# Sparse attention and an FFN on one core: attention pairs taken two to a slot, with one attention head of the slot

## The chip, the cores and the metric

The kernel runs on one core of a Trainium2 chip. Its metric is the device time of one execution in microseconds. A profile of one execution shows when each engine worked: PE (TensorE, matmuls and transposes), DVE (VectorE), ACT (ScalarE), POOL (GpSimd) and SP (SyncE, which here only issues DMAs; POOL issues DMAs too).

## The reference

Attention over q, k, v of 8 batches, 8 heads, 576 positions and 64 elements, then an FFN on the 4608 tokens of 512 features that it gives. Heads 0 to 3 see a window of 32 positions, heads 4 to 7 every 32nd position.

```python
scores = scale * np.matmul(q, k.transpose(0, 1, 3, 2))
rel = pos[:, None] - pos[None, :]
mask_local = (rel >= 0) & (rel < stride)                                   # heads 0 to 3
mask_strided = (rel >= 0) & (pos[None, :] % stride == pos[:, None] % stride)   # heads 4 to 7
scores = np.where(masks, scores, -1e9)
attn = softmax(scores)
x = (attn @ v), heads side by side          # 4608 x 512
h = (x @ w1) * (x @ w2) @ w3                # d_ff = 1024
out = h @ w_out                             # 4608 x 512, float32
```

## The kernel before

**Work and its units.** Two heads of a batch make a pair, 32 in all, four to a batch: pairs 0 and 1 of a batch are local, 2 and 3 strided. A pair goes through these steps, each a function:

- `load_qk` and `load_v` bring q, k and v in (q and k, and the strided v, through POOL's queue; the local v through SP's). `emit_cast_v` casts the local v on POOL, and `shift_v` makes a copy of it that is shifted by 32 rows, with two DMAs on SP's queue.
- `emit_T`: TensorE transposes q and k (36 transposes for a local pair, 44 for a strided one) into the two PSUM buffers of pool `psA`; the copies to SBUF go to ACT, but the strided q goes to DVE.
- `emit_S`: scores (36 or 22 small matmuls) into two buffers of `psF`, and the mask added by two DVE operations.
- `emit_max`, `emit_sub` (DVE), `emit_exp` (ACT), `emit_norm`: sum and reciprocal on DVE (L371, L373), product on POOL (L374).
- `emit_P`: the probabilities transposed. `by_dma` decides: strided pairs from `XB` = 8 on use a DMA transpose on SP's queue (L388), the others TensorE (`pp`, 5 transposes for a local pair, 6 for a strided one) and a copy on ACT.
- `emit_V`: probabilities times v (36 or 22 matmuls) into two `psF` buffers, copied into `xT` by ACT, and for strided pairs by ACT once and DVE twice.

The FFN works on 9 chunks of 512 tokens. w3 and w_out are folded into one matrix `wfh` at the start. `emit_a` and `emit_b` are four matmuls of 128x512 each, eight times per chunk; ACT copies the result of a to `asb`, DVE multiplies it with that of b into `abt` (L256). `emit_out` makes a tile of 128 tokens with eight matmuls; ACT copies it to `osb` and SP sends it.

`psF` has six buffers (PSUM banks) for scores, values and all FFN results; a new tile takes the bank that was released first.

**Order.** The program's order is written out by hand, engine by engine in the order of the calls (`tc.manual_schedule()`). Pairs 0 to 8 have a prologue of single calls. From pair 9 on a loop does one step for each pair n:

```python
for n in range(9, NP + 2):
    ...
    if by_dma(n - 1):
        emit_P(n - 1)
    ...
    emit_S(n); emit_V(n - 2); emit_T(n + 1)      # one attention block on TensorE
    feed(0.1 * f, first)                          # f = 5.2
    emit_max(n); feed(...); emit_sub(n); emit_exp(n); feed(...)
    ...
```

`feed` puts FFN pieces in between: it adds its microseconds to a credit and emits pieces (0.87 for an a or b, 1.74 for an output tile) until the credit is used up; `next_piece` decides which, and only from batches that are done (`first`, `full`). An output tile of a chunk may come when two more pieces of the next chunk are out, or when no a or b is possible. When the loop ends, `feed(1e9, B)` emits all that is left.

Of the kernel before, what the change touches and what calls it, by code (L numbers as in the profile page):

```python
# [27 lines left out]
def kernel(  # L28
# [11 lines left out]
    nc = tc.nc  # L40
# [30 lines left out]
    NP, XB = 4 * B, 8  # L71
    staged, cast, qks, prs, pts = {}, {}, {}, {}, {}
# [143 lines left out]
    abts, aqs = {}, {}  # L216
# [41 lines left out]
    def emit_out(c, ts):  # L258
        ps = psF.tile([P, DM], FP32, tag="f", name="ops")
        for jc in range(KC2):  # L260
            nc.tensor.matmul(ps, abts[c][:, jc, ts * P:(ts + 1) * P], wfh[:, jc, :],  # L261
                             start=(jc == 0), stop=(jc == KC2 - 1))
        osb = ffn.tile([P, DM], FP32, tag="osb", bufs=3, name="osb")
        nc.scalar.copy(out=osb, in_=ps)  # L264
        nc.sync.dma_start(out_r[c * (NT // P) + ts], osb)

# [16 lines left out]
    def emit_T(i, qeng=nc.scalar.copy):  # L283
# [4 lines left out]
        tps = [psA.tile([P, nsl, npar], FP16, tag="tr", name=f"tp{n}") for n in "qk"]  # L288
# [6 lines left out]
        if local:  # L295
            kT = kTL[par]
            qT = att.tile([P, LB, HALF], FP16, tag="qT", name="qT")
            for dst, off, tp in ((qT, 0, tps[0]), (kT, QB, tps[1])):
                eng = qeng if dst is qT else nc.scalar.copy
                eng(out=_sub(dst, 0, P, off, [[LB, HALF], [1, LB]]),  # L300
                    in_=_sub(tp, 0, P, 0, [[1, HALF], [HALF, LB]]))
        else:
            qT = qTS[par]
            kT = att.tile([P, ST * SW], FP16, tag="kT", name="kT")
            nc.vector.tensor_copy(out=qT[:, :, 0:SW], in_=tps[0])
            nc.scalar.copy(out=kT, in_=tps[1].rearrange("p t k -> p (t k)"))
        qks[i] = (qT, kT)

    def emit_S(i):

        b, hp, local, par = where(i)
        qT, kT = qks.pop(i)
        nt, w = (LB, LW) if local else (ST, SW)
        tmp = att.tile([P, nt, w], FP32, tag="tmp", name="tmp")
        n1 = 5 if local else 6
        sps = [psF.tile([P, n, w], FP32, tag="f", name="sp") for n in (n1, nt - n1)]
        for s in [x for u in range(n1) for x in (u, n1 + u) if x < nt]:
            bank, t = divmod(s, n1)
            for h in range(2):
# [10 lines left out]
                nc.tensor.matmul(sps[bank][c:c + HALF, t, :], qT[r, T, :], kT[r, SW * T:SW * T + w], start=True, stop=True)  # L330
        for bank, (t0, t1) in enumerate(((0, n1), (n1, nt))):
            if local:
                msk = maskL[:, 0:5, :] if t0 == 0 else maskL[:, 1:5, :]
            else:
                msk = _sub(maskS, 0, P, 0, [[0, t1 - t0], [1, SW]])
            nc.vector.tensor_tensor(out=tmp[:, t0:t1, :], in0=sps[bank], in1=msk, op=ALU.add)  # L336
        prs[i] = tmp

# [27 lines left out]
    def emit_norm(i):  # L366
# [6 lines left out]
        nc.vector.reciprocal(out=rc, in_=sm)  # L373
        nc.gpsimd.tensor_tensor(out=prv, in0=prv, in1=_sub(rc, 0, P, 0, [[1, nt], [0, w]]),  # L374
                                op=ALU.mult)

# [22 lines left out]
    def emit_V(i):  # L399
        b, hp, local, par = where(i)  # L400
        vv, pT = pts.pop(i)
        x0 = S * b
        if local:
            ops = [psF.tile([P, LC - half, HALF], FP32, tag="f", name="op") for half in range(2)]
# [12 lines left out]
            for half in range(2):  # L417
                nc.scalar.copy(out=_sub(xT[hp], 0, P, x0 + HALF * half,
                                        [[P, LC - half], [1, HALF]]), in_=ops[half])
        else:  # L420
            ops = [psF.tile([P, 6 - half, SW], FP32, tag="f", name="op") for half in range(2)]
            for s in range(6):
                for half in range(2):
# [3 lines left out]
                    for h in range(2):  # L427
# [5 lines left out]
            nc.scalar.copy(out=_sub(xT[hp], 0, P, x0, [[NR, NA], [11, 3], [1, 6]]),  # L433
                           in_=_sub(ops[0], 0, P, 0, [[3, NA], [1, 3], [SW, 6]]))
            nc.vector.tensor_copy(out=_sub(xT[hp], 0, P, x0 + 6, [[NR, NA], [11, 2], [1, 5]]),
                                  in_=_sub(ops[1], 0, P, 0, [[3, NA], [1, 2], [SW, 5]]))
            nc.vector.tensor_copy(out=_sub(xT[hp], 0, P, x0 + 28, [[NR, NA], [1, 4]]),  # L437
                                  in_=_sub(ops[1], 0, P, 2, [[3, NA], [SW, 4]]))
# [6 lines left out]
    T_A = 0.87  # L445
    state = {"credit": 0.0, "ab": 0, "out": 0, "turn": 0}

    def next_piece(batches):
# [5 lines left out]
        can_out = oc < NCH and a >= 2 * KC2 * (oc + 1) + (0 if c >= NCH else 2)  # L454
# [38 lines left out]
    with tc.manual_schedule():  # L493
# [186 lines left out]
        for n in range(9, NP + 2):  # L680
            full = (n - 1) // 4
            first = full - 1 if n % 4 == 1 else full
            f = 5.2
            if n + 4 < NP:
                load_qk(n + 4)
            for i in (n + 3, n + 2):
                if i < NP and where(i)[2] == (i == n + 3):
                    load_v(i)
            if by_dma(n - 1):
                emit_P(n - 1)  # L690
            if n < NP:
                shift_v(n)
            if n < NP:
                emit_S(n)
            emit_V(n - 2)
            if n + 1 < NP:
                emit_T(n + 1)
            feed(0.1 * f, first)
            if n < NP:
                emit_max(n)  # L700
            feed(0.15 * f, first)
            if n < NP:
                emit_sub(n)
                emit_exp(n)
            feed(0.15 * f, full)
            if n <= NP and not by_dma(n - 1):
                emit_P(n - 1)
# [38 lines left out]
```

## Time and profile before

| | |
|---|---|
| median of 3 runs | 281.21 us (280.95 to 281.38) |
| the profiled execution | 281.55 us, of which the profile's span is 279.8 |
| PE busy | 263.6 us, 94% |
| DVE, ACT, POOL busy | 172.4, 150.5, 159.1 us |
| chain that ended last | PE 66%, DMA 8%, POOL 7%, issue 7%, DVE 6%, ACT 3% |

A line of the profile names the source line, engine and operation, the written and read tiles, the shape and the count. Busy time is that of the engine. In order of time the first number is the start in us from the span's start, the second the length, and in brackets stand the idle time before it and what ended that. A matmul's length is that of its way through the array; successive matmuls overlap, so TensorE's pace is read from one start to the next.

### The profile page before, as it was taken

Reading aid. Unit: us, or ns where it says so; the run is one execution under the profiler, and the core shown is the slowest. Engines: PE = TensorE matmul, PEld = TensorE weight load, DVE = VectorE, ACT = ScalarE, POOL = GpSimd, SP = SyncE. Lnnn points to the kernel's source line nnn. Section 1 sums busy time; section 2 is a strip of 40 time slices with the busy share of each in tenths; the row PEclk is TensorE's granted clock in tenths of the full one; section 3 lists DMA queues with packets and bytes.
Section 4 is the critical chain, followed back from the end, with each engine's and each line's share of the span. In section 5 each row is a group of like instructions: output and inputs, shape, how many; then the busy total and the mean of one; then the engine's idle time right before and its main releaser. Section 6 shows DMA issues by size and latency. Waiting matters only on the chain.

```text
span 279.8 us, 10171 instructions
## 1 busy us (share of the span) xinstructions
PE 263.6 (94%) x4355; PEld 138.4 (49%) x4355; DVE 172.4 (62%) x342; ACT 150.5 (54%) x270; POOL 159.1 (57%) x242
## 2 busy tenths in 40 slices
PE   6479988899999999999999999999999999999994
PEld 6436545454555555545554555455455544444441
DVE  3515664498778867876777688587867841331310
ACT  3324466457676666655675666576656534324322
POOL 7763875779398588557757755895977110000000
PEclk9957999999999999999999999999999999999999
DMA  7999699979779599668957986995674213001113
GB/s 137 189 201 223 93 149 203 152 132 200 157 144 196 75 195 232 71 102 199 229 67 110 224 178 74 166 226 96 75 185 87 30 45 135 0 0 53 63 62 125
DMA packets 59981, 36.95 MB, mean 132 GB/s; under 512 B 38180, under 2 KB 54304, under 8 KB 59936
## 3 DMA queue, kind: packets, MB, share of 16 engines
q0 software_dynamic: 23392, 17.29, 43.3%
q1 hardware_dynamic: 36544, 19.01, 26.6%
q8 instruction: 34, 0.56, 0.8%
q14 instruction: 11, 0.09, 0.1%
HBM read 39.24 MB, written 9.44 MB: 174 GB/s over the span
## 4 chain that ended last, share of the span: by engine, by line
PE 66%; DMA 8%; POOL 7%; issue 7%; DVE 6%; ACT 3%; SPq 1%; POOLq 0%; DVEq 0%; ACTq 0%
PE ops L261 19%; PE bps L253 17%; PE aps L243 16%; PE fps L233 4%; DMA vhL<-vhL 3%; DMA w3s<-in_moe_w_dram 3%; DMA pT<-prS 2%; POOL s L105 2%; DVE abt L256 2%; PE tpk L292 2%; PE tpq L292 1%; PE pp L393 1%; PE op L429 1%; POOL vhS L130 1%; PE op L413 1%
## 5 line engine op out<-in xcount | busy, mean ns | idle before, releaser
L256 DVE TENSOR_TENSOR abt<-bps,asb 128x512 f16<-128x512 f32 x72 | 49.4, 686 | 42.1 <-PE bps L253 39.9
L253 PE MATMUL bps<-xT,w2h 128*128 128x512 f16 x288 | 74.1, 380 | 0.0
L243 PE MATMUL aps<-xT,w1h 128*128 128x512 f16 x288 | 74.0, 379 | 0.0
L261 PE MATMUL ops<-wfh,abt 128*128 128x512 f16 x288 | 65.5, 379 | 0.0
L247 ACT COPY asb<-aps 128x512 f32<-128x512 f32 x72 | 42.2, 587 | 33.9 <-PE aps L243 33.7
L264 ACT COPY osb<-ops 128x512 f32<-128x512 f32 x36 | 21.1, 587 | 42.6 <-PE ops L261 40.3
L261 PEld LDWEIGHTS <-abt 128*128 128x128 f16 x288 | 27.4, 98 | 32.0
L130 POOL DMA_DIRECT2D vhS<-in_v_dram x70 | 42.0, 665 | 1.1 <-issue 1.1
L253 PEld LDWEIGHTS <-w2h 128*128 128x128 f16 x288 | 26.8, 98 | 30.4
L243 PEld LDWEIGHTS <-w1h 128*128 128x128 f16 x288 | 27.0, 98 | 29.6 <-DVE xT L437 0.4
L374 POOL TENSOR_TENSOR prS<-prS,rc 128x594 f16<-128x594 f16 x16 | 19.5, 1220 | 37.0 <-ACT asb L247 26.1
L374 POOL TENSOR_TENSOR prL<-prL,rc 128x576 f16<-128x576 f16 x16 | 19.0, 1187 | 18.5 <-DVE rc L373 16.9
L351 DVE TENSOR_TENSOR tmp<-tmp,mx 128x576 f32<-128x576 f32 (+1 forms) x32 | 25.5, 797 | 1.0
L105 POOL DMA_DIRECT2D s<-in_k_dram x35 | 22.5, 719 | 3.9 <-DMA w2h<-in_moe_w_dram 2.9
L344 DVE TENSOR_REDUCE mx<-tmp 128x9 f32<-128x576 f32 (+1 forms) x32 | 24.0, 752 | 0.2
L233 PE MATMUL fps<-woh,w3T 128*128 128x512 f16 x64 | 18.8, 426 | 4.2 <-issue 1.6
L105 POOL DMA_DIRECT2D s<-in_q_dram x35 | 21.7, 654 | 1.5 <-DMA w1h<-in_moe_w_dram 1.5
L336 DVE TENSOR_TENSOR tmp<-sp,maskL 128x320 f32<-128x320 f32 (+1 forms) x32 | 13.1, 450 | 13.8 <-PE sp L324 13.8
L292 PE MATMUL tpq<-id,s 54*64 54x54 f16 (+1 forms) x640 | 17.1, 194 | 2.3 <-DMA s<-in_q_dram 2.3
L371 DVE TENSOR_REDUCE sm<-prL 128x9 f32<-128x576 f16 x16 | 12.0, 753 | 10.8 <-ACT prL L363 10.8
L292 PE MATMUL tpk<-id,s 54*64 54x54 f16 (+1 forms) x640 | 17.7, 195 | 0.2
L292 PEld LDWEIGHTS <-s 54*64 54x64 f16 (+1 forms) x1280 | 14.8, 108 | 6.0 <-DMA s<-in_q_dram 2.9
(75 smaller groups left out, 296.8 us busy)
## 6 DMA issues: line engine op xcount, KB each, us to landing
out_dram<-osb SPq DMA_DIRECT2D x36, 256.0 KB, 3.1
vsL<-in_v_dram SPq DMA_DIRECT2D x32, 128.0 KB, 4.9
s<-in_k_dram POOLq DMA_DIRECT2D x16, 144.0 KB, 4.1
s<-in_q_dram POOLq DMA_DIRECT2D x16, 144.0 KB, 3.9
s<-in_q_dram POOLq DMA_DIRECT2D x31, 74.2 KB, 4.6
s<-in_k_dram POOLq DMA_DIRECT2D x31, 74.2 KB, 4.9
w3s<-in_moe_w_dram POOLq DMA_DIRECT2D x4, 512.0 KB, 10.2
vhL<-vhL SPq DMA_DIRECT2D x16, 120.0 KB, 5.2
```

What stands on the lines that cost most here:

```text
L105: nc.gpsimd.dma_start(t[p0 + r0[0]:p0 + r0[1], h, 0:n * D], _ap(src[b, h0 + h], 0 + ap[0], ap[1] + [[1, n * D]]))
L130: nc.gpsimd.dma_start(vt[HALF * half + r0[0]:HALF * half + r0[1], h, 0:m * D], _ap(v[b, h0 + h], 6 * half * D + ap[0], ap[1] + [[1, m * D]]))
L233: nc.tensor.matmul(ps, w3T[:, kc, :], woh[:, kc, :], start=(kc == 0), stop=(kc == KC2 - 1))
L243: nc.tensor.matmul(aps, w1h[:, ci, jc * P:(jc + 1) * P], xT[ci][:, c * NT:(c + 1) * NT], start=(ci == 0), stop=(ci == KC1 - 1))
L247: nc.scalar.copy(out=asb, in_=aps)
L253: nc.tensor.matmul(bps, w2h[:, ci, jc * P:(jc + 1) * P], xT[ci][:, c * NT:(c + 1) * NT], start=(ci == 0), stop=(ci == KC1 - 1))
L256: nc.vector.tensor_mul(abts[c][:, jc, :], bps, abts.pop((c, jc)))
L261: nc.tensor.matmul(ps, abts[c][:, jc, ts * P:(ts + 1) * P], wfh[:, jc, :], start=(jc == 0), stop=(jc == KC2 - 1))
L292: nc.tensor.transpose(tp[HALF * h:HALF * h + HALF, s, :], s16[p0:p0 + npar, h, s * D:(s + 1) * D], id16[p0:p0 + npar, p0:p0 + npar])
L344: nc.vector.tensor_reduce(out=mx, in_=tmp, axis=AX.X, op=ALU.max)
L351: nc.vector.tensor_tensor(out=tmp, in0=tmp, in1=_sub(mx, 0, P, 0, [[1, nt], [0, w]]), op=ALU.subtract)
L374: nc.gpsimd.tensor_tensor(out=prv, in0=prv, in1=_sub(rc, 0, P, 0, [[1, nt], [0, w]]), op=ALU.mult)
```

## The change

The step for each pair is replaced from pair 11 on. `emit_T`, `emit_S`, `emit_norm` and `emit_V` are split into their matmuls and the copies or operations that follow (`mm_T`, `evict_T`, `mm_S`, `emit_mask`, `emit_sum`, `emit_div`, `mm_V`, `evict_V`). A slot takes a local and a strided pair together, and a string `STEADY` gives the order of its calls: first letter the step, second letter the pair (L or S), and at the end the engine of a copy (a for ACT, d for DVE); f and g are feeds of 0.29. `now` is the slot's two pairs (scores to probabilities), `old` those of the slot before (values), `new` those of the next (q and k transposed), `far` those three slots on (q and k loaded). On TensorE a slot starts with S of the local pair, T of the next strided pair, S of the strided pair, T of the next local pair, V of the strided old pair, V of the local old pair, with no FFN pieces between them. T of the strided pair uses `psF` (`TSB`), T of the local one `psA` (`TLA`). In a slot the copy of a strided q goes to ACT and that of a local k to DVE.

Pairs 9 and 10 have calls of their own; T of pair 12 is among them. `XB` = 11 takes pair 10 from the DMA transpose to TensorE. `LAG` = 4 lets output tiles come two pieces later. The last output tile is made in two halves of 256 columns, with buffers of their own, the first copied by DVE and the second by ACT, and sent by a DMA each.

```diff
-    NP, XB = 4 * B, 8
+    NP, XB = 4 * B, 11
...
     def emit_out(c, ts):
-        ps = psF.tile([P, DM], FP32, tag="f", name="ops")
-        for jc in range(KC2):
-            nc.tensor.matmul(ps, abts[c][:, jc, ts * P:(ts + 1) * P], wfh[:, jc, :],
-                             start=(jc == 0), stop=(jc == KC2 - 1))
-        osb = ffn.tile([P, DM], FP32, tag="osb", bufs=3, name="osb")
-        nc.scalar.copy(out=osb, in_=ps)
-        nc.sync.dma_start(out_r[c * (NT // P) + ts], osb)
-
+        rows = out_r[c * (NT // P) + ts]
+        last = c == NCH - 1 and ts == NT // P - 1
+        for n, w in enumerate((DM // 2, DM // 2) if last else (DM,)):
+            ps = psF.tile([P, w], FP32, tag="f", name="ops")
+            for jc in range(KC2):
+                nc.tensor.matmul(ps, abts[c][:, jc, ts * P:(ts + 1) * P],
+                                 wfh[:, jc, n * w:n * w + w], start=(jc == 0),
+                                 stop=(jc == KC2 - 1))
+            osb = ffn.tile([P, w], FP32, tag="osb" if w == DM else "osl", bufs=3 if w == DM else 2,
+                           name="osb")
+            (nc.vector.tensor_copy if last and n == 0 else nc.scalar.copy)(out=osb, in_=ps)
+            nc.sync.dma_start(rows[:, n * w:n * w + w], osb)
...
-    def emit_T(i, qeng=nc.scalar.copy):
+    def mm_T(i, space=psA, tag="tr"):
 
         b, hp, local, par = where(i)
         nsl, npar = (LB, HALF) if local else (ST, SW)
         s16 = cast.pop(i)
-        tps = [psA.tile([P, nsl, npar], FP16, tag="tr", name=f"tp{n}") for n in "qk"]
+        tps = [space.tile([P, nsl, npar], FP16, tag=tag, name=f"tp{n}") for n in "qk"]
...
+    def evict_T(i, which="qk", eng=None):
+
+        b, hp, local, par = where(i)
+        tps = qks[i]
+        for c in which:
+            tp = tps["qk".index(c)]
+            e = eng or (nc.vector.tensor_copy if c == "q" and not local else nc.scalar.copy)
+            if local:
+                dst, off = ((att.tile([P, LB, HALF], FP16, tag="qT", name="qT"), 0) if c == "q"
+                            else (kTL[par], QB))
+                e(out=_sub(dst, 0, P, off, [[LB, HALF], [1, LB]]),
+                  in_=_sub(tp, 0, P, 0, [[1, HALF], [HALF, LB]]))
+            elif c == "q":
+                dst = qTS[par]
+                e(out=dst[:, :, 0:SW], in_=tp)
+            else:
+                dst = att.tile([P, ST * SW], FP16, tag="kT", name="kT")
+                e(out=dst, in_=tp.rearrange("p t k -> p (t k)"))
+            qts.setdefault(i, {})[c] = dst
+
+    def emit_T(i, qeng=None):
+        mm_T(i)
+        evict_T(i, "q", qeng if where(i)[2] else None)
+        evict_T(i, "k")
...
+    def banks_V(i):
+        local = where(i)[2]
+        n, w = (LC, HALF) if local else (6, SW)
+        vops[i] = [psF.tile([P, n - half, w], FP32, tag="f", name="op") for half in range(2)]
...
+    def evict_V(i, half, eng=nc.scalar.copy):
+        b, hp, local, par = where(i)
+        x0, ops = S * b, vops[i]
+        if local:
+            eng(out=_sub(xT[hp], 0, P, x0 + HALF * half, [[P, LC - half], [1, HALF]]),
+                in_=ops[half])
+        elif half == 0:
+            eng(out=_sub(xT[hp], 0, P, x0, [[NR, NA], [11, 3], [1, 6]]),
+                in_=_sub(ops[0], 0, P, 0, [[3, NA], [1, 3], [SW, 6]]))
+        else:
+            eng(out=_sub(xT[hp], 0, P, x0 + 6, [[NR, NA], [11, 2], [1, 5]]),
+                in_=_sub(ops[1], 0, P, 0, [[3, NA], [1, 2], [SW, 5]]))
+            eng(out=_sub(xT[hp], 0, P, x0 + 28, [[NR, NA], [1, 4]]),
+                in_=_sub(ops[1], 0, P, 2, [[3, NA], [SW, 4]]))
...
+    T_A, T_F, LAG = 0.87, 0.29, 4
+    STEADY = ("bL SL mL TSB tSka SS mS xS TLA VS vS1d VL tSqa vS0a uS xL g lLq vL1a g "
+              "lLk g cL hL f f eS lSq g g uL g g vL0a f eL f tLkd g rS f tLqa dS f f wL "
+              "PS f f f f rL f f g f f g f f g dL f g f f f PL lSk f f wS f g ").split()
...
-        can_out = oc < NCH and a >= 2 * KC2 * (oc + 1) + (0 if c >= NCH else 2)
+        can_out = oc < NCH and a >= 2 * KC2 * (oc + 1) + (0 if c >= NCH else LAG)
...
-        for n in range(9, NP + 2):
-            full = (n - 1) // 4
-            first = full - 1 if n % 4 == 1 else full
-            f = 5.2
-            if n + 4 < NP:
-                load_qk(n + 4)
-            for i in (n + 3, n + 2):
-                if i < NP and where(i)[2] == (i == n + 3):
-                    load_v(i)
-            if by_dma(n - 1):
-                emit_P(n - 1)
-            if n < NP:
-                shift_v(n)
-            if n < NP:
-                emit_S(n)
-            emit_V(n - 2)
-            if n + 1 < NP:
-                emit_T(n + 1)
-            feed(0.1 * f, first)
-            if n < NP:
-                emit_max(n)
-            feed(0.15 * f, first)
-            if n < NP:
-                emit_sub(n)
-                emit_exp(n)
-            feed(0.15 * f, full)
-            if n <= NP and not by_dma(n - 1):
-                emit_P(n - 1)
-            feed(0.2 * f, full)
-            if n < NP:
-                emit_norm(n)
-                if n + 1 < NP:
-                    emit_cast_v(n + 1)
-            feed(0.4 * f, full)
+        load_qk(13)
+        load_v(12)
+        load_v(11)
+        shift_v(9)
+        emit_S(9)
+        emit_V(7)
+        emit_T(10)
+        load_qk(14)
+        emit_max(9)
+        feed(0.78, 1)
+        emit_sub(9)
+        emit_exp(9)
+        feed(1.04, 2)
+        emit_norm(9)
+        feed(1.04, 2)
+        emit_P(8)
+        feed(2.34, 2)
+        emit_S(10)
+        emit_V(8)
+        emit_T(11)
+        load_qk(15)
+        mm_T(12, psF, "f")
+        evict_T(12, "q", cp)
+        evict_T(12, "k", act)
+        emit_max(10)
+        feed(0.78, 2)
+        emit_sub(10)
+        emit_exp(10)
+        feed(1.04, 2)
+        emit_norm(10)
+        feed(1.04, 2)
+        emit_P(9)
+        load_qk(16)
+        feed(2.04, 2)
+        emit_P(10)
+        feed(0.30, 2)
+        for a in range(11, NP + 1, 2):
+            new, far, old = {}, {}, {}
+            now = {"LS"[not where(i)[2]]: i for i in (a, a + 1) if i < NP}
+            for d, off in ((old, -2), (new, 2), (far, 6)):
+                d.update({"LS"[not where(i)[2]]: i for i in (a + off, a + off + 1) if i < NP})
+            full = (a - 1) // 4
+            first = full - 1 if a % 4 == 1 else full
+            turn = 0
+            for op in STEADY:
+                c, t, x = op[0], op[1:2], {"a": act, "d": cp}.get(op[-1])
+                if c == "f" or c == "g":
+                    feed(T_F, full if c == "f" else first)
+                elif c in "SmxuerdPch":
+                    if t in now:
+                        {"S": mm_S, "m": emit_mask, "x": emit_max, "u": emit_sub, "e": emit_exp,
+                         "r": emit_sum, "d": emit_div, "P": emit_P, "c": emit_cast_v,
+                         "h": shift_v}[c](now[t])
+                elif c == "b":
+                    banks_V(old[t])
+                elif c == "V":
+                    mm_V(old[t])
+                elif c == "v":
+                    evict_V(old[t], int(op[2]), x)
+                elif c == "T" and t in new:
+                    if op[2] == "A":
+                        mm_T(new[t])
+                    else:
+                        mm_T(new[t], psF, "f")
+                elif c == "t" and t in new:
+                    evict_T(new[t], op[2], x)
+                elif c == "w" and t in new:
+                    load_v(new[t])
+                elif c == "l" and t in far:
+                    load_qk(far[t], op[2])
+        emit_V(NP - 1)
         feed(1e9, B)
```

`mm_S` with `emit_mask`, `emit_sum` with `emit_div`, and `mm_V` hold the lines that `emit_S`, `emit_norm` and `emit_V` had.

## The prediction

> **What bounds the kernel now.** I read the page first, then TensorE's matmuls in order of time, then VectorE's. The page:
>
> ```profile
> PE 263.6 (94%) x4355; PEld 138.4 (49%) x4355; DVE 172.4 (62%) x342; ACT 150.5 (54%) x270; POOL 159.1 (57%) x242
> PEclk9957999999999999999999999999999999999999
> ```
>
> TensorE is the only engine near its span, at full clock from the fifth slice on. From 76 us it has work in every view, so time moves only by what is put into or taken out of its stream. In order of time, two attention blocks between FFN pieces (four matmuls of 512 columns; neighbouring pieces start 0.865 us apart):
>
> ```profile
> 120.95 1.03 PE L243 MATMUL aps<-xT,w1h 128*128 128x512 f16 x4
> 121.91 0.45 PE L324 MATMUL sp<-kTL,qT 64*32 64x64 f16 x36
> 122.74 0.37 PE L429 MATMUL op<-pT,vhS 54*64 54x54 f16 x22 [0.39 <-DMA pT<-prS]
> ...
> 123.38 1.04 PE L253 MATMUL bps<-xT,w2h 128*128 128x512 f16 x4
> ...
> 140.94 1.03 PE L243 MATMUL aps<-xT,w1h 128*128 128x512 f16 x4
> 141.90 0.37 PE L330 MATMUL sp<-kT,qTS 64*64 64x54 f16 x22
> 142.08 0.47 PE L413 MATMUL op<-pT,vhL 64*64 64x32 f16 x34
> ...
> 142.86 1.04 PE L253 MATMUL bps<-xT,w2h 128*128 128x512 f16 x4
> ```
>
> A block costs the start of the next piece minus the end of the last: 142.86-140.94-0.86 = 1.06 us undisturbed, 123.38-120.95-0.86 = 1.57 where V waits for the DMA transpose. Four undisturbed blocks (1.11, 1.17, 1.12, 1.06) make 4.46 a batch, 2.23 for two pairs. Above that lie 0.45 (block at 121.6), 0.22 (173.6), 0.31 (199.6), 0.32 (212.9) and 0.10 (109.5): 1.4 us of waits.
>
> The transposes, in the view of line L388:
>
> ```profile
> L388 SPq DMA_TRANSPOSE pT<-prS x12: 1221/1372/2024, 90.8 to 227.3; - x12
> DMA to landing us min/median/max: 2.5/4.5/6.0
> ```
>
> VectorE in order of time, from the score block of pair 10 (starting 84.05) to its reciprocal:
>
> ```profile
> 84.84 0.83 DVE L336 TENSOR_TENSOR tmp<-sp,maskS 128x324 f32<-128x324 f32 x2
> 85.59 0.46 DVE L305 COPY qTS<-tpq 128x594 f16<-128x594 f16 x1
> 85.96 0.76 DVE L344 TENSOR_REDUCE mx<-tmp 128x11 f32<-128x594 f32 x1
> 86.75 0.78 DVE L351 TENSOR_TENSOR tmp<-tmp,mx 128x594 f32<-128x594 f32 x1
> 87.45 0.69 DVE L256 TENSOR_TENSOR abt<-bps,asb 128x512 f16<-128x512 f32 x1
> 88.36 0.77 DVE L371 TENSOR_REDUCE sm<-prS 128x11 f32<-128x594 f16 x1 [0.22 <-ACT prS L363]
> 89.23 0.23 DVE L373 RECIPROCAL rc<-sm 128x11 f32<-128x11 f32 x1
> ```
>
> Durations overlap their successor by about 0.1, so I count start to start: mask pair 0.75, copy 0.37, max 0.79, subtract to exp 0.88, exp to sum 0.73, sum 0.87, reciprocal to the GpSimd product (89.61) 0.38, product to its user (90.81) 1.20.
>
> **Part 1, joined blocks.** From pair 11 a slot does S of the local pair, T, S of the strided pair, T, V, V without FFN matmuls between. From matmul starts: entry 0.09; S 0.25 and 0.18; T 0.39 and 0.31; V 0.18 and 0.32; exit 0.11; five switches at 0.065 (block at 147.8: 1.11 less its own parts 0.98, over two switches). Sum 2.17 against 2.23: -0.06, in ten slots -0.6. At the end the blocks at 219.8 (0.71) and 225.7 (0.40) become one of about 1.0: -0.1. The old waits: loads go out six pairs ahead instead of four, and the transpose is issued in its own slot (part 3). I take all 1.4 away; if none goes, add it back.
>
> **Part 2, what the joined block waits for.** Six PSUM banks serve S, T (one T now sits there too) and V. In the changed kernel's order of instructions the second bank of the local V is that of the strided S's first bank, free after the mask add. From the slot's first S matmul: local mask pair at 0.53 (121.91 to 122.44), strided mask at 0.53+0.74 = 1.27, its first half (0.49) done 1.76, seen by TensorE at about 1.82. TensorE alone would be there at 1.67. So 0.15 a slot, behind it the other 34 V matmuls and all FFN pieces: +1.5 over ten slots. Bounds: nothing (release seen at once, T slower), 0.3 a slot where VectorE enters late.
>
> The local K copy moves from ScalarE to VectorE (757 ns, the row of the three Q copies there) and the strided Q copy (457) the other way: +0.30 us on VectorE a slot, which is 19.8 us busy in each 26 us. In slots that end in three output pieces, VectorE's list, start to start, is: masks to 2.13, max 0.69, V copies 0.40, subtract 0.70, max 0.69, two products 1.22, subtract 0.70, K copy 0.66, so the strided sum starts at 7.19 and its reciprocal 0.87 later at 8.06; after 0.14, two products (1.22) and the local sum (0.87) the local reciprocal starts at 10.29, and GpSimd's product runs from 10.67 to 11.87. TensorE wants that P after 2.23 (the block and its wait, from the first S) +7x0.865+2x1.73 = 11.75. With 0.06 for the semaphore 0.17 a slot, four such slots (15, 19, 23, 27): +0.7. Bounds 0 and 0.4.
>
> **Part 3, the transpose in its slot.** It goes out at 8.06+0.38+1.20 = 9.64 in these slots and 8.51 in the others, and V of the next slot wants it at 15.4 and 13.5 (slots of 14.04 and 12.13 us). That leaves 5.8 and 5.0 us against a landing of 2.5 to 6.0, median 4.5, and the slot's loads are mostly landed by then. Cost zero; without that cover up to 1.0 in each of five slots.
>
> **Part 4, pair 10.** Its P goes back from a DMA to TensorE: six transposes, 0.28 for five (the block at 86.6) plus 0.056: 0.34. But this P stands between FFN pieces soon after its own S. VectorE now also copies Q of pair 12 (0.757, 0.66 start to start) ahead of the max. From the S start: mask 0.79, copies 1.54 and 1.91, max 2.57, subtract 3.36, exp 4.24, sum 4.97, reciprocal 5.84, product 6.22, P possible at 7.45. TensorE arrives after the block (1.03 plus 0.31 for pair 12's T, moved here), five pieces (4.33) and one P (0.28): 5.95. Wait 1.5. Bounds 0.8 (before, the product ended at 6.73 after S; with no copy in the way that is still late) and 1.8. In all +1.84.
>
> **Part 5, last tile.** 16 matmuls of 256 columns take what 8 of 512 did. The last copy falls from 587 to 378 ns (the 128x256 row of L418): -0.21. The final transfer shrinks from 256 to 128 KB; out of 3.1 us from the last copy's end to the span's end I give 0.1 (bounds 0 and 0.6, as rows of 32 KB also take 4 to 5 us under load): -0.3. The Trainium skill (DMA: Bandwidth & Descriptors, "Anatomy of one DMA") fits GpSimd's transfers with 2.0 us plus bytes over 436 GB/s, an estimate of 0.30 less for half the bytes; by it the part is -0.5.
>
> **At no cost:** GpSimd's reordered loads (some ten issues of 0.63 to 0.72, two products of 1.2 and a cast of 0.73 come to 9.9 us of a 13 us slot); SP's value loads ahead of the transpose and outputs behind it (outputs have three buffers; without that cover one late issue, up to 2.0, holds the next output copy); outputs starting two FFN pieces later. VectorE doing the first half of the last tile is off the path, 0.4 beside 0.86 of matmuls.
>
> Sum: -0.6-0.1-1.4+1.5+0.7+1.84-0.3 = +1.6. The profiled execution took 281.55 (span 279.8), so 283.2; the median of the runs, 281.21, lies 0.34 lower: **282.8**.
>
> **Rivals.** *The waits fade (faster).* All three new waits hang on one chain, VectorE's from mask to reciprocal. For it: TensorE had only 1.4 us of waits so far, with VectorE as loaded. Against it: the start-to-start rows. It decides when strided mask's first half is free by 1.67 after the slot starts and pair 10's product comes by 6. Without any: 282.8-1.5-0.7-1.5 = 279.1; with half of pair 10's left, 279.9.
>
> *Nothing measurable.* Only the V and P waits go: 280.6; with half of them left 281.7.
>
> *Transposes land late.* At 6.0 in slots with 5.0 of room, V stalls 1.0 in five slots and a little in the others: 282.8+5 = 288 at worst, 284.5 to 286 when one to three are late. For it: this transfer already stalled TensorE three times. Against: fewer loads run beside it.
>
> *The clock drops.* A joined block is 2.3 us without wide matmuls. For a price: at 17 us wide matmuls start 427 ns apart instead of 216, through 23; each such 6 us would lose 3, so one drop gives 286. Against: a 2.24 us block at 76.0 left the clock at 1.00. The Trainium skill (TensorE: Matmul & The Clock Gate, Part 1) says that an idle window of about 3.4 us halves the clock, and Part 4 that transposes do not count as busy in the same way; by that two neighbouring blocks would have to merge, and the row agrees with no drop.
>
> **Chances.** The forecast's case 0.50 (own range 281.8 to 284.2), waits fade 0.22, nothing measurable 0.12, transposes late 0.14, clock 0.02. Range 279.3 to 285.3: it leaves out the best of the first rival and the worst of the last two. About 0.2% (0.56 us) is what a measurement of this kernel can tell from no change: faster 0.22, same 0.13 (its case, and 0.01 from the forecast's edge), slower 0.65.
>
> **What would show it.** Right: TensorE idle before pair 10's P for 1 to 1.8 us, released by GpSimd's product; the second V bank's matmul waiting on the mask add in each slot; joined blocks of 2.3; no V wait on a transpose. Wrong: blocks near 2.17 or less, P of pair 10 not waiting, or V of the strided pair waiting for DMA.

## The result and the profile after

The changed kernel took 288.63 us (median of four runs, 288.35 to 288.69) against 281.08 us before: a ratio of 1.0267, 95% interval 1.0249 to 1.0285. The prediction had said 282.8, with a range to 285.3. The direction was right and the size was not: the sum gave +1.6 us, the two profiled executions (281.55 and 288.69) show +7.1.

Page of the profile after:

```profile
PE 267.2 (93%) x4369; PEld 142.1 (50%) x4369; DVE 174.7 (61%) x345; ACT 149.5 (52%) x271; POOL 158.1 (55%) x242
PEclk9958899999999999999999999999999999999999
q8 instruction: 34, 0.56, 0.8%
```

The clock is full from the sixth of 40 slices on. TensorE is "busy" 3.6 us more with 14 matmuls more. The profile models the ends of matmuls, so busy time says little here, and I go by starts. Its timeline, a joined block (slot 19; a slot is named after its first pair):

```profile
146.52 0.45 PE L342 MATMUL sp<-kTL,qT 64*32 64x64 f16 x36
...
147.27 0.35 PE L348 MATMUL sp<-kT,qTS 64*64 64x54 f16 x21
...
147.85 0.42 PE L471 MATMUL op<-pT,vhS 54*64 54x54 f16 x22
148.21 0.58 PE L459 MATMUL op<-pT,vhL 64*64 64x32 f16 x36
148.76 1.02 PE L253 MATMUL bps<-xT,w2h 128*128 128x512 f16 x4
```

The last wide matmul ahead of it starts at 146.21, so the block costs 148.76-146.21-0.21 = 2.34 us, and six of the ten (slots 15 to 25) cost the same to 0.01. The sum said 2.32. No V matmul in the joined slots waits for a transpose, and the median landing of the transposes is 2.5 us where it was 4.5.

The P of pair 10, timeline of TensorE:

```profile
88.15 0.45 PE L433 MATMUL pp<-id,prL 128*128 128x128 f16 x5 [0.24 <-POOL prL L410]
...
89.30 1.03 PE L243 MATMUL aps<-xT,w1h 128*128 128x512 f16 x4
92.04 0.51 PE L433 MATMUL pp<-id,prS 128*128 128x128 f16 x6 [1.72 <-POOL prS L410]
```

The wait for GpSimd's product is there, 1.9 us by starts (1.5 predicted). The P of pair 9 ahead of it, which did not wait before, now costs 0.69 instead of 0.28.

Two things that no line of the sum has. The first, on VectorE and GpSimd in slot 19 (its first S starts at 146.52):

```profile
148.66 0.77 DVE L375 TENSOR_REDUCE mx<-tmp 128x11 f32<-128x594 f32 x1
...
149.73 1.59 DVE L382 TENSOR_TENSOR tmp<-tmp,mx 128x594 f32<-128x594 f32 x1
151.25 0.74 DVE L375 TENSOR_REDUCE mx<-tmp 128x9 f32<-128x576 f32 x1
```

```profile
149.60 1.09 POOL L276 CAST vhL<-vsL 128x640 f16<-128x640 f32 x1
150.26 1.56 POOL L105 DMA_DIRECT2D s<-in_q_dram  x2
```

Up to the subtract every start is where the prediction's list has it (masks to 2.13, max 0.69, V copies 0.40: 3.22 after S; it is 3.21). Then the subtract takes 1.52 to the next start, not 0.70: GpSimd's cast of v has started 0.13 us ahead of it. The same happens in slots 15 (length 1.45) and 23 (1.58), and to the subtract of pair 10 beside pair 9's product (1.60). Before, the length was 0.78 in all of these. In the three slots the subtract ends 1.72 us after the cast's start, whether it started 0.13 or 0.27 behind it: 0.77 of its own after some 0.95. Behind it everything on VectorE is 0.7 to 0.8 late: output tiles wait for `abt` by 0.29, 0.44 and 0.42 us in slots 15, 19 and 23, and the local P in each of these by 0.33. One of these waits, in slot 19:

```profile
156.75 1.04 PE L264 MATMUL ops<-wfh,abt 128*128 128x512 f16 x4 [0.21 <-DVE abt L256]
```

The second, TensorE in slot 27, in the local pair's transposes:

```profile
200.96 0.19 PE L296 MATMUL tpk<-id,s 64*64 64x64 f16 x1
...
202.50 0.22 PE L296 MATMUL tpq<-id,s 64*64 64x64 f16 x2 [1.17 <-issue]
202.64 0.37 PE L471 MATMUL op<-pT,vhS 54*64 54x54 f16 x22
202.83 0.52 PE L459 MATMUL op<-pT,vhL 64*64 64x32 f16 x36
```

TensorE stands for 1.2 us in the middle of a block, and the profile names nothing that releases it: "issue". Slot 11 has another behind its joined block (1.0 us, between two wide matmuls of one piece):

```profile
96.67 0.38 PE L253 MATMUL bps<-xT,w2h 128*128 128x512 f16 x1
97.89 0.82 PE L253 MATMUL bps<-xT,w2h 128*128 128x512 f16 x3 [0.84 <-issue]
```

The trace has 8,765 TensorE instructions, and the page lists 34 transfers of the instruction queue (q8) with 0.56 MB: 16 KB each, so some 256 instructions. Counted in program order both stalls stand at the same place modulo 256. A joined block has 392 instructions (196 matmuls, each with its weight load) in 2.1 us, so two of these instruction-block ends can fall into one, 1.4 us apart.

Hence the theories: **port** (a VectorE subtract of two SBUF inputs and a GpSimd operation that reads SBUF exclude each other), **instruction blocks** (a second block end that follows the first too closely finds its instructions not yet there), and pair 10's P as predicted.

### The profile page after: what moved, and what is told of

Read it like the earlier page. It is cut to its first block, busy times and chain, and to the rows that moved or that the text cites. A ratio compares the mean times of both kernels' runs of the same rounds, so it can differ in the third digit from the quotient of the medians.

```text
span 287.0 us, 10192 instructions
## 1 busy us (share of the span) xinstructions
PE 267.2 (93%) x4369; PEld 142.1 (50%) x4369; DVE 174.7 (61%) x345; ACT 149.5 (52%) x271; POOL 158.1 (55%) x242
## 3 DMA queue, kind: packets, MB, share of 16 engines
q1 hardware_dynamic: 35888, 18.82, 23.9%
## 4 chain that ended last, share of the span: by engine, by line
PE 70%; DVE 11%; issue 5%; DMA 5%; POOL 4%; ACT 4%; SPq 0%; DVEq 0%; POOLq 0%; ACTq 0%
PE aps L243 18%; PE ops L264 18%; PE bps L253 18%; PE fps L233 5%; DVE abt L256 3%; DMA w3s<-in_moe_w_dram 3%; DVE tmp L363 2%; PE pp L433 2%; DMA vhL<-vhL 2%; PE tpq L296 2%; PE op L459 2%; PE sp L342 2%; POOL prL L410 2%; DVE mx L375 1%; DVE tmp L382 1%
## 5 line engine op out<-in xcount | busy, mean ns | idle before, releaser
L256 DVE TENSOR_TENSOR abt<-bps,asb 128x512 f16<-128x512 f32 x72 | 48.4, 681 | 40.0 <-PE bps L253 39.7
L264 PE MATMUL ops<-wfh,abt 128*128 128x512 f16 (+1 forms) x296 | 66.6, 374 | 0.6 <-DVE abt L256 0.4
L269 ACT COPY osb<-ops 128x512 f32<-128x512 f32 (+1 forms) x36 | 20.9, 580 | 48.5 <-PE ops L264 41.6
L264 PEld LDWEIGHTS <-abt 128*128 128x128 f16 x296 | 28.1, 98 | 32.3 <-DVE abt L256 2.5
L382 DVE TENSOR_TENSOR tmp<-tmp,mx 128x576 f32<-128x576 f32 (+1 forms) x32 | 28.1, 879 | 0.4
L105 POOL DMA_DIRECT2D s<-in_q_dram x35 | 23.0, 729 | 3.1 <-DVE s L97 2.5
L105 POOL DMA_DIRECT2D s<-in_k_dram x35 | 21.5, 645 | 2.3 <-DVE s L97 1.0
L436 ACT COPY pT<-pp 128x640 f16<-128x640 f16 (+1 forms) x21 | 15.1, 717 | 6.0 <-PE pp L433 6.0
L296 PEld LDWEIGHTS <-s 54*64 54x64 f16 (+1 forms) x1280 | 14.0, 108 | 6.1 <-issue 3.8
L296 PE MATMUL tpk<-id,s 54*64 54x54 f16 (+1 forms) x640 | 17.0, 194 | 0.0
```

The source lines that it names most:

```text
L105: nc.gpsimd.dma_start(t[p0 + r0[0]:p0 + r0[1], h, 0:n * D], _ap(src[b, h0 + h], 0 + ap[0], ap[1] + [[1, n * D]]))
L256: nc.vector.tensor_mul(abts[c][:, jc, :], bps, abts.pop((c, jc)))
L296: nc.tensor.transpose(tp[HALF * h:HALF * h + HALF, s, :], s16[p0:p0 + npar, h, s * D:(s + 1) * D], id16[p0:p0 + npar, p0:p0 + npar])
L382: nc.vector.tensor_tensor(out=tmp, in0=tmp, in1=_sub(mx, 0, P, 0, [[1, nt], [0, w]]), op=ALU.subtract)
```

## The experiments

All times of one row are from one chip; the kernel before took 281.6 to 282.1 us (medians) there, with more spread than in the first runs. For shares I use a second number, worked out from each profile: the time from the 121st wide feed-forward matmul (in the changed kernels just ahead of pair 9's P, at 87 us) to the end of the span. It leaves out the start, whose loads vary by 2 us from run to run. In the three kernels without the change (before, halves_only, best_before) that matmul stands right behind pair 9's P instead, so their number lacks 0.28. The ratios of cast_early, load14, no_stall, fill_p10, all_three, swapV and best_after have intervals that overlap or touch that of the changed kernel: what each of them shows, it shows in the profile of one execution.

| kernel | ratio to before (95%) | 121st to end, us |
|---|---|---|
| before | 1 | 192.7 |
| changed | 1.0267 (1.0249 to 1.0285) | 200.1 |
| changed, again | 1.0283 (1.0243 to 1.0322) | 200.4 |
| cast_early | 1.0261 (1.0210 to 1.0311) | 198.9 |
| load14 | 1.0243 (1.0199 to 1.0286) | 199.4 |
| shift64 | 1.0805 (1.0752 to 1.0857) | 219.3 |
| no_stall | 1.0218 (1.0188 to 1.0249) | 199.9 |
| fill_p10 | 1.0262 (1.0223 to 1.0302) | 200.3 |
| all_three | 1.0218 (1.0178 to 1.0258) | 197.9 |
| swapV | 1.0318 (1.0279 to 1.0358) | 201.5 |
| p10_dma | 1.0448 (1.0405 to 1.0492) | 206.5 |
| best_after | 1.0220 (1.0176 to 1.0265) | 197.4 |
| halves_only | 1.0002 (0.9974 to 1.0029) | 192.7 |
| best_before | 0.9963 (0.9928 to 0.9998) | 191.9 |

**cast_early**

```diff
-"... uS xL g lLq vL1a g lLk g cL hL f f ..."
+"... uS xL g cL lLq vL1a g lLk g hL f f ..."
```

> The changed kernel with GpSimd's cast of v issued one step earlier in each slot (ahead of the q and k loads instead of behind them), so that it ends before VectorE's strided subtract starts. Theory (a subtract of two SBUF inputs and a GpSimd operation that reads SBUF stop each other): the strided subtract of slots 15, 19, 23, 27 goes from 1.59 back to about 0.78 us, the cast from 1.09 to about 0.73, the waits of output tiles for abt in those slots (0.5 to 0.85 us each) shrink to under 0.15 and the waits of the local P fall from 0.6 to about 0.45; 1.5 us faster than the changed kernel (287.1, between 286.5 and 287.9). Rival (the subtract is slow because its input was just written, or by its shape; the cast is only beside it): the subtract stays at 1.59 and the time at 288.6.

VectorE and GpSimd in the same slot 19:

```profile
149.16 0.77 DVE L375 TENSOR_REDUCE mx<-tmp 128x11 f32<-128x594 f32 x1
...
150.25 0.77 DVE L382 TENSOR_TENSOR tmp<-tmp,mx 128x594 f32<-128x594 f32 x1
150.93 0.75 DVE L375 TENSOR_REDUCE mx<-tmp 128x9 f32<-128x576 f32 x1
```

```profile
148.93 1.07 POOL L276 CAST vhL<-vsL 128x640 f16<-128x640 f32 x1
149.59 0.95 POOL L100 DMA_DIRECT2D s<-in_q_dram  x1
```

The subtract is back at 0.77. The output tiles wait no more in slots 15, 19 and 23 (before 1.15 us in all), nor does the local P (before 0.99): 2.1 us. That the cast made the subtract slow is shown; that the two exclude each other is an inference, which the 1.72 us above fits. Beside GpSimd's load issues the subtract keeps its 0.77, so those are not the cause. The cast's own 1.07 did not shrink: it reads so in both kernels, while the next GpSimd instruction starts 0.66 behind it in both, so the cast was never the loser. The forecast of 1.5 us less was missed: the second number falls by 1.2, since in the profiled execution slot 11's stall had grown from 1.0 to 1.8 us and took 0.8 back, and the ratio, 1.0261, can't be told from 1.0267.

**load14**

```diff
-        load_qk(14)
...
         emit_norm(9)
+        load_qk(14)
```

> The changed kernel with the q and k loads of pair 14 issued behind pair 9's product on GpSimd instead of ahead of it. Theory: pair 9's product starts some 2.7 us earlier and no longer runs beside VectorE's subtract of pair 10, which goes from 1.60 to about 0.78; pair 9's P (0.69) waits no more (0.28), pair 10's product ends 0.8 us earlier; its P still waits some 1.5 us. 0.8 us faster than the changed kernel (287.8, between 287.3 and 288.2). Rival (pair 10's product is late by its own chain of VectorE steps, whose length does not depend on GpSimd): pair 9's P is 0.4 shorter, pair 10's P waits 0.4 longer, and the time stays at 288.6.

Pair 9's product starts at 83.88 instead of 86.89, the subtract of pair 10 is 0.78, pair 9's P costs 0.28 again. Pair 10's P costs 2.2 as before: the steps now start where the prediction's list has them, to 0.01 us, up to GpSimd's product (6.22 after S), but that product, behind the load issues put in its way, takes 1.59 us instead of 1.18. So the rival (pair 10's P waits longer by what pair 9's P gains) did not come. The second number falls by 0.75 as forecast, but partly by luck: 0.40 is pair 9's P, and 0.47 is slot 11's stall, which came out at 0.5 instead of 1.0 and which the move did not aim at.

**shift64**

```diff
-    def warm(n):
+    def warm(n, narrow=0):
...
+        for s in range(narrow):
+            nc.tensor.matmul(ps[:, s % 4, 0:8], wz, wz[:, 0:8], start=True, stop=True)
...
-        warm(16)
+        warm(16, 32)
```

> The changed kernel with 32 matmuls of 8 columns (64 TensorE instructions) added in the warm-up, in a stretch where TensorE waits 2 us for a weight load; nothing else is changed. Theory (TensorE takes its instructions in blocks of 256, and where two block ends fall within one joined block of some 390 small instructions the second block is not there yet): the stall of about 1.2 us, called issue, leaves slot 27 (and slot 29's 0.3), stays in slot 11, and comes up in the joined blocks of slots 13, 15 and 17, perhaps also 19 and 21; none in 23 to 29. The time goes up by 2.4 to 4.8 us against the changed kernel, to 291 to 293.4. Rival (the stalls of slots 11 and 27 are waits for a semaphore or a transfer that the trace does not show): the same two slots stall and the time stays within 0.3 of 288.6.

The places came as expected, all of them: stalls in slots 11, 13, 15, 17, 19 and 21, all six at one place modulo 256, within two instructions, none in 23 to 29. The sizes did not: 2.0, 3.5, 2.8, 3.3, 1.6 and 2.1 us. Slot 17 on TensorE, and the clock row:

```profile
149.02 0.52 PE L459 MATMUL op<-pT,vhL 64*64 64x32 f16 x29
152.66 0.34 PE L459 MATMUL op<-pT,vhL 64*64 64x32 f16 x7 [3.12 <-issue]
152.93 3.60 PE L264 MATMUL ops<-wfh,abt 128*128 128x512 f16 x8
```

```profile
PEclk9958999999999797979879999999999999999999
```

The trace has the 16 KB transfer for the missing block at 150.28 to 151.16, 2.4 us after TensorE passed the first block end, and TensorE goes on 1.5 us after it has landed. Then comes a second cost: eight wide matmuls span 3.60 us, 427 ns from start to start instead of 213. After four of the stalls (blocks of 4.5 to 6.2 us without a wide matmul) 6 to 12 matmuls ran at half pace, 7.2 us in all. So 64 instructions in the warm-up, in TensorE's idle time, cost 15 us by the ratios, where 2.4 to 4.8 were forecast. (The profiled execution took 309.4 us against a median of 304.5, so its second number is some 5 too high, and the sizes of its stalls may be.)

**no_stall**

```diff
     def warm(n):
...
+        if n == 56:
+            for s in range(12):
+                nc.tensor.matmul(ps, wz, ...)    # 512 columns
+            n = 8
...
-                        mm_T(new[t], psF, "f")
+                        mm_T(new[t], psF, "f", {11: 18, 17: 12, 21: 18}.get(a, 0))
```

> The changed kernel with the ends of TensorE's 256-instruction blocks moved so that no joined block and none of the 40 instructions behind it holds two of them: 36 warm-up matmuls fewer (48 of 128 columns are put into 12 of 512), and 18, 12 and 18 repeated 64x64 transposes in slots 11, 17 and 21. Theory (a second block end within a joined block stalls TensorE): the stalls of slots 11 (1.0), 27 (1.2) and 29 (0.3) are gone and no slot from 11 on has a new one; the repeats cost some 0.5; 2.0 us faster than the changed kernel (286.6, between 286 and 287.4). Rival (the stalls belong to the places in the program, slot 27's transposes and slot 11's feed-forward matmuls, and shift64 only added others): the stalls stay where they were, 289.

The last argument of `mm_T` is the number of transposes that it repeats. Slot 27, TensorE:

```profile
201.20 0.19 PE L350 MATMUL sp<-kT,qTS 64*64 64x54 f16 x1
...
201.61 0.42 PE L473 MATMUL op<-pT,vhS 54*64 54x54 f16 x22
201.97 0.58 PE L461 MATMUL op<-pT,vhL 64*64 64x32 f16 x36
202.52 0.81 PE L253 MATMUL bps<-xT,w2h 128*128 128x512 f16 x3
```

The stalls of slots 11 and 27 are gone, and no slot has a new one. Slot 29's block stays at 2.62, so its 0.3 was none. The instruction-block theory is shown from both sides. Less is won than the 2.0 us forecast, 1.4 by the ratios and 0.2 in the second number: the repeats cost 1.0 in all instead of 0.5, and in the first feed-forward stretch, where the shift took another such stall away (block at 47 us: 4.0 in the kernel before, 3.2 in the changed one, 2.2 here), TensorE then reached an earlier local P (at 61.9) and pair 9's P ahead of GpSimd's products, which stood behind its loads, and waited 1.1 and 1.2 us more.

**fill_p10** (on no_stall)

```diff
-        feed(2.04, 2)
+        feed(3.6, 2)
         emit_P(10)
-        feed(0.30, 2)
+        feed(0.00, 2)
```

> no_stall with 1.56 us more of feed-forward matmuls ahead of pair 10's P (feed 3.6 in place of 2.04, none behind it). Theory (its wait of 1.9 is for GpSimd's product, which ends when it ends, so that work put in front hides it): the P's wait falls to 0.3 or less, and the time by 1.5 us against no_stall. Rival (the feed-forward work put in front delays VectorE's and ScalarE's steps of pair 10 by its own products, so that the wait moves along, or slot 11's own steps come late): under 0.5 us.

P of pair 10 waits no more. But from slot 11 on the feed-forward work runs ahead of VectorE: 0.8 at 100.66, 0.5 at 110.11, 0.2 in slot 15's block, 0.3 at 137.80, 1.0 more at the P at 144.4, released mostly by VectorE's `abt` and V copies. The wait moved along: the rival held. Nothing was won against no_stall (0.4 more in the second number, 1.2 in the medians), so TensorE's order at pair 10 is not what costs: VectorE is late there.

**all_three** (fill_p10 with cast_early and load14)

> fill_p10 with GpSimd's cast of v one step earlier (cast_early) and pair 14's loads behind pair 9's product (load14). Theory (collisions between GpSimd's and VectorE's operations, 2.1 us by cast_early's profile and 0.4 of pair 9's P): 2.4 us less than fill_p10, so that with the two others the changed kernel loses nearly all of its 7.5 and lies within 1.5 us of the kernel before (281 to 283). Rival (the collisions only fill time that another wait would take): under 0.8 us less than fill_p10.

2.5 less than fill_p10 in the second number, 1.5 in the medians. That part held. The forecast of 281 to 283 did not (287.69), as no_stall and fill_p10 had brought next to nothing. By the profile, 1.0 us of what is left is the repeats, 0.6 a stall at an instruction-block end in pair 9's P, and the waits that fill_p10 brought at 0.8, 0.5, 0.3 and 1.0 are all still there.

**swapV**

```diff
-TLA VS vS1d VL tSqa
+TLA VL VS vS1d tSqa
```

> The changed kernel with the local pair's V matmuls ahead of the strided pair's in each slot. The prediction put 0.15 us per slot on the second PSUM bank of the local V, which waits for VectorE's strided mask add. Theory (TensorE waits for that bank at whichever V comes second in line): with the local V first its banks are asked for earlier still, its wait grows and no time is won; joined blocks 2.3 to 2.5 us. Rival (only the order is at fault, the strided V could run in that time): joined blocks 2.17 to 2.2 us, 1 to 1.2 us less in all.

Joined blocks stay at 2.34: TensorE still waits for banks, whichever V is first, so this order does not help. How much of the 2.34 is waiting is better read in the changed kernel's slot 27, where the other engines had time during the stall: from the first strided V to the next wide matmul 0.64 us (202.64 to 203.28) against 0.91 in slot 19. So 0.27 is waiting and 2.07 the block itself, where the sum had 0.15 and 2.17. Start by start against slot 27, only about half of the 0.27 has VectorE's mask add as its releaser (0.04 and 0.09); the other half is ScalarE's copies of the strided k (0.10, ahead of the first local V) and q (0.04, ahead of the wide matmul), which the sum did not have. The kernel came out 1.4 us slower than the changed one by the ratios; in its profile slot 27's block is 3.55 us, and seven wide matmuls behind it run at half pace, 1.5 us.

**p10_dma**

```diff
-    NP, XB = 4 * B, 11
+    NP, XB = 4 * B, 10
```

> The changed kernel with pair 10's P transposed by DMA, as in the kernel before, instead of on TensorE (XB 10). Part 4 of the prediction put 1.84 us on that P's way over TensorE; the changed kernel shows 2.2 us for it, of which 1.9 is a wait for GpSimd's product. Theory (the product ends when it ends, and the pair's V stands 5 us behind it): the 2.2 us at that P are gone, and the strided V of slot 11 waits for the transpose instead, 1.5 to 3 us, so the sum changes by less than 1 us. Rival (the transpose lands in time): 2.0 us faster. The 12 instructions fewer move the block ends: slot 11's stall gets shorter, one of about 1 us stays in slot 27.

Waits of TensorE:

```profile
PE op L471 <- DMA pT<-prS: 6.2, 1, 6.2
```

and SyncE's queue:

```profile
91.76 2.43 SPq L428 DMA_TRANSPOSE pT<-prS  x1
```

The 2.2 us at the P are gone, and V of slot 11 waits 6.2 for the transpose, issued at 91.76 and awaited until 98.65. Worse than either theory: 5 us slower than the changed kernel by the ratios, with ten wide matmuls at half pace (2 us) behind the 8.9 us block, and a stall of 0.9 in slot 25 that was not forecast, beside the forecast one of 0.9 in slot 27. Given this order of pairs, TensorE was the cheaper way for pair 10.

**after_again**

> The changed kernel once more, as it is, beside the three others. Theory: its stalls without a named releaser stand at the same instructions as in the first profile (slot 11 behind its fifth-last block end, slot 27 in its transposes) and its strided subtracts of slots 15, 19 and 23 take 1.45 to 1.6 us again; 288.6 against 281.5. Rival (both come by chance in one execution): other places or sizes in this profile.

Same places: 0.9 in slot 11, 0.9 in slot 27, subtracts of slots 15 to 23 late with output tiles waiting 0.31, 0.45, 0.44. Slot 29's block was 0.45 longer in this one, at an "issue" again.

**best_after** (cast_early, load14, ten repeats in slot 23)

> The changed kernel with cast_early's and load14's moves and 10 repeated transposes (20 instructions) in slot 23, which put the block ends of slots 25 to 29 back where slots 21 to 25 had theirs without a stall. Theory: cast_early takes 2.1 off, load14 0.7, the stall of slot 27 1.2, the repeats cost 0.2; 3.7 us faster than the changed kernel (285, between 284.2 and 286), still 3 us slower than the kernel before by slot 11's stall, pair 10's P and the joined blocks. Rival (what is taken off comes back as another wait, as in fill_p10): within 1 us of the changed kernel.

3.0 us less than the changed kernel beside it in the second number, 1.9 in the medians (287.65 against 289.51), where 3.7 was forecast. Slot 27's block is 2.34 and every P of the joined slots but slot 27's costs 0.28 to 0.31; slot 11's stall (0.9) is left, and another at an instruction-block end, 0.9 at 112.29 in slot 13, which is 0.3 in the changed kernel.

**halves_only** and **best_before** (the kernel before with the last tile in halves; the second with the 36 fewer warm-up matmuls too)

> The kernel before with only the last output tile in two column halves, as in the change. By the change's own tail (3.49 us from the last tile's first matmul to the end against 4.15 before) 0.6 us faster than the kernel before (280.5); by the sum of the prediction 0.3 faster (280.8); rival (the two output stores of half the size end no earlier than the one, and the shorter tail came from the DMA rings being emptier): no difference, 281.1.

> The kernel before with the last output tile in halves and with 36 warm-up matmuls fewer (48 of 128 columns put into 12 of 512), which moves the block ends. Its own profile has one stall without a releaser, of 1.6 us, in the first feed-forward stretch (at 47.7 us), and no pair of block ends less than 3.2 us apart behind that. Theory (that stall is one of the block ends too, and went in no_stall): it is gone here, but the steps behind it wait for GpSimd and for loads, as they did in no_stall, so that most of it comes back: 0 to 1 us faster than the kernel before, plus 0 to 0.6 by the halves. Rival: the whole 1.8 is won, 279.5.

Halves alone make no difference that the runs can tell. In the profile the last copy's start to the end of the last transfer falls from 2.28 to 1.75 us, as in the changed kernel, but the span ends 2.19 after that transfer instead of 1.41. (The 3.49 and 4.15 of the expectation are counted from the start of the last matmul, which is half as wide in the change, so 0.11 of their difference is no gain.) Three kernels (these two and p10_dma) have 2.19, all others 1.41 to 1.44; why was not tried. best_before lost its stall at 47 us (4.0 to 2.2), but nothing of that is left in its profile at the 121st matmul: it reached the stretch 2.2 us later, after two waits of 1.8 us each for loads of v between 23 and 27 us. Its 0.8 less in the second number is waits of V for the DMA transpose (1.1 us in the kernel before, none here), against 0.2 more at the end. It is 0.37% faster than the kernel before, the interval just off 1, and the only version of which that can be said; what makes it so is not shown.

## Why the prediction was wrong, step by step

*Held.* The reading of TensorE as the only engine whose stream sets the time. The joined block, 2.34 against 2.32, but by luck that close: the block itself was 0.10 shorter (2.07, not 2.17), the wait for the mask add about as forecast (0.13 for 0.15), and 0.14 of waiting for ScalarE's copies, which the sum did not have, filled the gap. The transposes in their own slot at no cost. The wait at pair 10's P and its releaser. Of the signs named for "right" all four came, and the forecast was still 5.5 us short: none of them looks at what was left out.

*Parts 1 and 2, blocks and old waits:* -0.5 predicted for the ten slots. The old blocks of these pairs add up to 23.8 us, the new ones without stalls to 23.9: +0.1. (Slot 13's block reads 2.62, but holds pair 12's P, 0.28, which stood by itself before.) The difference is in slots 11 and 29, taken to be like the rest: slot 11 (2.55) waits longer for the mask add at both V's (0.25 and 0.21 from start to start), and slot 29 (2.62, with only one T) waits 0.4 for ScalarE's copy of k. The old waits for transposes did go, but their 1.4 us are those of one execution: of them only 0.3 is in best_before's profile.

*Part 2, VectorE's list, "subtract 0.70":* the step that failed, together with the missing term below. It came out at 1.38 to 1.52 in three slots. The local P paid 0.33 instead of 0.17 there, and the output tiles, which the sum did not look at, 1.15. The list carried durations over from a kernel in which GpSimd was doing something else at that moment. "At no cost: GpSimd's reordered loads, products and a cast" added up GpSimd's time and did not look at what stands beside what. The Trainium skill (SBUF — State Buffer, "Who interferes with whom") has the rule: a VectorE instruction with two SBUF inputs and a GpSimd instruction that reads SBUF exclude each other, and whoever starts first holds the port for its whole length. Here that agrees: 0.78 becomes 1.59 where the cast had started 0.13 us earlier, and 0.77 again where it was gone. The prediction did not weigh it.

*Part 4, pair 10:* +1.84 predicted, 2.23 measured, and 0.41 more at pair 9's P. Both excesses, 0.8 in all, come from one collision: pair 9's product, late behind four load issues, against pair 10's subtract. The sum had 3.36 to 4.24 for that subtract and exp; the next step stood 0.82 later. load14 took the collision away and half of the 0.8 with it; the other half went into the longer product.

*Part 5, last tile:* -0.3 predicted; the last transfer ends 0.5 earlier. The copy's 0.21 was right. For the transfer I gave 0.1; it is 0.3. The -0.5 by the Trainium skill's fit (DMA: Bandwidth & Descriptors, "Anatomy of one DMA") was the better figure, though the fit is given for GpSimd's transfers and this one is SyncE's.

*No term at all:* the instruction blocks, 2.4 us in slots 11 (1.0), 27 (its block costs 1.1 more than the others) and 13 (0.3, at 112.17). The trace of before could have given a warning: its one "issue" stall stands at the same place modulo 256, and the spacing of block ends can be counted for both kernels. By the starts in the two traces, no two ends behind 50 us are under 4 us apart in the kernel before; in the changed one five pairs are under 3 (slot 27's 1.2 before its stall, the others 2.0 to 2.9), and with the program moved in steps of four instructions every position has three or more, down to 1.1. Spacing alone does not decide: 2.7, 2.9 and 2.0 passed in slots 23, 25 and 29, while slot 11's 2.7 and slot 13's 3.9 stalled. What decides is when the 16 KB transfer lands. Each trace has 34 of them and 34 block ends; I take them in order, the first transfer with the second end and so on, 462 pairs in the 14 traces. In 41 pairs the transfer landed less than 1.2 us before TensorE came to the end, or after it: at all 41 TensorE stalled, and went on 1.2 to 1.6 us after the landing. In the other 421 it landed 1.3 us or more ahead, and there is no such stall. The transfers of slots 23, 25 and 29 had begun 1.0 to 1.5 us before the previous end, that of slot 11 began 1.4 behind it. What makes one begin early is not shown.

*Rivals.* None was it. "The clock drops" did not happen in the change, but did in swapV, shift64 and p10_dma. The Trainium skill (TensorE: Matmul & The Clock Gate, Part 1) puts the idle window at about 3.4 us; that agrees: the changed kernel's longest block, 3.4 in slot 27, kept the clock, and swapV's 3.55 there lost it, though some 2 us of each were small matmuls and transposes, not idle time.

What the sum lacked: stalls 2.4, output tiles 1.15, local P 0.5, pairs 9 and 10 0.8, blocks 0.6, and 0.4 in the last joined block and a gap behind it; less 0.25 in the tail. That makes 5.6 where 5.5 were missing. Such terms can't simply be taken off again: no_stall, fill_p10 and all_three took stalls and collisions away, and other waits came in their place.

## What to carry to other kernels

When a change moves work between slots, write the lists of VectorE and GpSimd side by side and mark every pair of operations that may not run together; a list of one engine with old durations is right only as far as its neighbour is. Count instructions too: a long run of small matmuls (here 256 instructions in 1.2 to 1.4 us) uses up its program faster than the next 16 KB arrive, and where the 256-instruction ends fall then matters, so that an unrelated edit ahead of it can cost several us. A filled wait is won only if the engine that released it has slack behind it.

## What was unexpected of the hardware

A stall at an instruction-block end was 0.2 to 3.5 us, at the one place behind slot 11's block 0.5 to 1.8 in six traces that have it there, with transfers of 0.9 to 1.75. The Trainium skill (Runtime: NRT & Kernel Launch, "Instruction fetch mechanics") calls the crossing of a 16 KiB boundary mostly hidden. That agrees for 421 of the 462 ends counted here, and does not for the 41 at which TensorE stood, shift64's six with up to 3.5 us among them.
